# A linear-attention and feed-forward block on one core: one more tile transposed by DMA, projections cut in two, the whole order rewritten

## The chip, the cores and the metric

The kernel runs on one core of one Trainium2 chip. A core has five engines that run side by side and meet through semaphores: TensorE (PE; its weight loads are shown as PEld), VectorE (DVE), ScalarE (ACT), GpSimd (POOL) and SyncE (SP, which here only issues DMAs; ACT issues a few too). Results of TensorE land in PSUM, eight banks of 512 fp32 columns per partition; everything else lies in SBUF. The metric is device time in microseconds (us), the median of several runs.

## The reference

One transformer block over 2048 tokens of width 640, in bf16:

```
h  = x + attention(layernorm(x)) @ wo
h2 = h + silu(layernorm(h) @ w1) @ w2        # hidden width 1728
attention: q, k, v = x @ wqkv, 32 heads of 20
  phi_q = [softmax(q w_phi), softmax(-q w_phi)]      (40 features per head)
  phi_k = the same of k
  kv = sum over tokens of phi_k^T v ;  z = sum of phi_k
  out = (phi_q kv) / (phi_q z)
```

The sums over all tokens (`kv`, `z`) must be complete before the first token's attention output can be formed, so the kernel has a key/value half and an output half.

## The kernel before, in words

The 2048 tokens are 16 tiles of 128. Tiles 0 to 3, 4 to 7, 8 to 11 and 12 to 15 share one transposed buffer `XnT` each. Nothing is scheduled by a planner at build time: the string `ORDER` is the program. Each word is a step, `name.arguments@banks`; a loop at the end of the kernel calls `op_name` with the arguments, and `banks` says which PSUM banks the step takes. Every engine executes its instructions in the order in which the words issue them. Waits for data, for a free PSUM bank and for a free buffer are set by the framework. SP's DMAs also take turns on eight completion semaphores, so each waits for the DMA eight places ahead of it.

The words that matter here (line numbers of the kernel before; `t` a tile, `g` a group of tiles):

- Loads: `lx` (x), `lk`, `lv` (key and value weights), `lp` (phi), `l1`, `l2`, `lh`, `lo` (later weights), all L236; `lq.c` (L251) loads and transposes a piece of the query weights.
- Warm-up: `wm` (L268) are products of constants whose results nobody reads.
- Weights: `wt.c` (L322) transposes a piece of the key weights on PE, `wc.c` copies it out of PSUM (`v` on DVE, `a` on ACT). `ph` (L198) spreads phi on DVE. `fk.c` (L337) multiplies both, so that the key projection gives `k w_phi` at once; `fc.c` casts the result into `Wfk` (L171 on ACT). `gk`, `gc` are the same for the query weights (`Wfq`).
- Layer norm of x: `st.t` (L273, L274) takes mean and variance on DVE, in two halves of 320 columns and an aggregation; `rs` (L278 to L289) makes the reciprocal root, a power on POOL (L281), and the shift (L283); `xn.t` normalises, on DVE (L297) or ACT (L302).
- Transposing x: either `xt.t` on PE (L308, five transposes) with a copy `xc.t`, or `xd.t`, one DMA transpose from SP (L315).
- Keys and values: `kp.t` and `vp.t` (L370), ten products each, 5 pieces of the contraction times 2 halves; `ke.t` (L395) takes both exponentials on ACT, `vc.t` copies the values. `kr.t` (L403, L406) sums and inverts on DVE, `kn.t` (L414, L418) multiplies, on POOL, or shared with DVE (`p` all on POOL, `q` three quarters, `b` half, `d` a quarter, `v` none). `cc.t` (L427) adds the tile to `kv`, 32 small products into bank 7.
- The join: `kc`, `km` (L441 to L445) turn `kv` into a block-diagonal operand `KVBD`, with the mask that `mc`, `mt` make.
- Queries: `qp`, `qs` (first part) and `qr`, `qt` (second part) are the products of four tiles with a piece of `Wfq` (L457), `qe` the exponentials on ACT (L479).
- Output of the attention: `dp.t` (L504), 40 small products into four banks; `dw.t` (L522 to L528) and `dr.t` (L533) divide on DVE; `do` scales (L539, POOL or DVE), `td.t` transposes by DMA (L559), `op.t` multiplies by `wo` (L566), `oa.t` adds to x (L575).
- Feed-forward: `sq`, `sr`, `hn`, `hd` normalise and transpose h; `up.g.k` (L645, L655) and `ua` (Silu, L667) make the hidden layer of a group of tiles, `yp`, `yh` (L691, L704) the second product, `yo` and `yz` add and store.

Two lines set the shape of the projections and of the statistics:

```
ps[:, half, 0:320], tok(XnT[t // GT], t)[:, c, :], W[:, c, half * 320 : (half + 1) * 320],
nc.vector.bn_stats(stats[:, k, :], X[:, t, k * 320 : (k + 1) * 320])
```

Of the kernel before, what the change touches and what calls it, by code (L numbers as in the profile page):

```python
# [31 lines left out]
rs.10.12 xn.8.a vc.2.a vc.1.a kp.2@0 ke.2 st.4 xd.9 st.5 kp.3@4 lo.0.2.s ke.3 rs.4.6 vp.3@2 xn.11.v vp.9@6  # L32
vc.9.a xn.4.a kp.9@0 ke.9 vc.3.a st.12 st.13 st.6 rs.12.14 xd.8 kr.1 kn.1.p kp.8@4 ke.8 mc.1 xn.13.a xn.12.a
xd.11 vp.11@6 vp.8@0 vc.8.a xn.5.v kr.0 kp.11@2 lq.2.s ke.11 st.7 rs.6.8 xn.6.a st.14 st.15 rs.14.16 xd.4
kr.9 vp.4@4 vc.4.a xd.5 vp.5@0 kn.0.p vc.11.a kr.2 vc.5.a kn.9.p kp.5@2 kr.11 kn.11.p gk.2@4 xn.10.a gc.2.a
xd.12 vp.12@6 vc.12.v kr.3 kn.3.p kp.4@0 xn.15.a ke.4 kp.12@4 cc.9 cc.1 kr.4 kn.4.p cc.0 xn.14.v cc.11 ke.5
kr.5 kn.2.d xd.13 ke.12 kr.12 lq.4.s xd.6 kp.6@0 lq.0.s ke.6 vp.13@2 vc.13.a kp.13@4 ke.13 vp.6@0 xd.15
xd.10 gk.4@2 vp.10@4 vc.6.a lq.3.s gk.3@0 gc.4.a gc.3.a vc.10.a kn.5.q kp.10@2 kn.12.p kr.6 xn.7.a l1.3.s
kn.6.q lq.1.s gk.1@0 gc.1.a kr.13 kn.13.p cc.4 cc.5 l1.0.s ke.10 kr.10 cc.2 cc.3 cc.12 xd.14 xd.7 kr.8
kn.8.p kn.10.d vp.15@4 vc.15.a kp.15@0 ke.15 kp.14@2 gk.0@4 gc.0.a vp.7@0 ke.14 kr.14 kn.14.p qp.0.1@4  # L40
# [6 lines left out]
dp.4@0 dw.4.p td.2 sq.0 qp.2.2@5 qs.2.2 qe.2.2 op.1@6 oa.1 sr.0 qp.2.1@4 dp.6@0 dw.6.p l1.5.s l1.1.s qs.2.1  # L47
qr.2.1 hn.0.a hd.0 sq.1 qt.2.1 sr.1 hn.1.v hd.1 qe.2.1 op.3@6 oa.3 sq.3 dp.5@0 dw.5.p op.2@4 sr.3 oa.2
hn.3.a sq.2 dr.5 do.5.0.p do.5.1.p qp.3.1@6 qs.3.1 l2.0.2.s l2.8.10.s qr.3.1 dp.9@0 dw.9.p td.5 dr.9
do.9.0.p dr.6 do.6.1.p dr.4 do.4.1.p do.4.0.p td.4 qt.3.1 qe.3.1 up.0.2@4 ua.0.2 dp.7@0 sr.2 up.0.0@6 ua.0.0  # L50
dw.7.p dr.7 up.0.3@4 ua.0.3 do.6.0.p dp.8@0 dw.8.p dr.8 hn.2.a up.0.1@6 ua.0.1 td.6 do.8.0.p op.5@4 oa.5
dp.12@0 dw.12.p dr.12 yp.1.0@6 do.7.1.p do.7.0.p sq.5 td.7 hd.3 op.4@4 oa.4 sr.5 hn.5.v hd.5 do.9.1.p sq.4
td.9 sr.4 hn.4.a dp.10@0 dw.10.p yp.1.1 yp.0.1@4 yh.0.0 hd.2 hd.4 yo.1 dp.11@0 dw.11.p dr.11 do.8.1.p
do.11.0.p td.8 yp.0.0 yo.0 op.7@6 oa.7 sq.7 dr.10 op.6@0 oa.6 sq.6 sr.6 op.9@2 up.1.6@4 do.11.1.v td.11 oa.9
sq.9 dp.15@0 ua.1.6 sr.9 up.1.5@6 ua.1.5 up.1.1@4 hn.9.v hd.9 do.10.0.p dw.15.p dr.15 hn.6.v hd.6 op.8@6
oa.8 sq.8 op.11@0 ua.1.1 sr.7 hn.7.v hd.7 up.1.3@2 oa.11 do.12.1.p sr.8 hn.8.v do.15.0.p dp.14@4 dw.14.p
dr.14 do.14.0.v hd.8 ua.1.3 up.1.4@0 ua.1.4 do.14.1.v td.14 up.1.0@2 sq.11 sr.11 hn.11.v ua.1.0 up.2.6@4
ua.2.6 dp.13@0 dw.13.p dr.13 do.13.1.p up.2.0@6 up.2.5@4 ua.2.5 op.14@0 up.1.2@2 ua.2.0 oa.14 sq.14 up.2.2@4
ua.1.2 do.12.0.p td.12 sr.14 op.12@6 oa.12 ua.2.2 hn.14.v do.10.1.p do.15.1.v yp.4.0@0 up.2.4@2 ua.2.4 td.10
op.10@4 oa.10 up.2.1@6 sq.12 sr.12 hn.12.a hd.11 hd.12 up.2.3@2 ua.2.1 yp.2.0@4 ua.2.3 yp.9.0@6 do.13.0.p  # L60
td.13 hd.14 yh.2.1@2 td.15 yh.1.0 yp.2.1 yo.2 yp.9.1 yo.9 op.13@4 yp.4.1 yo.4 sq.10 sr.10 yp.6.0@6 op.15@0
hn.10.v hd.10 oa.15 sq.15 sr.15 oa.13 hn.15.a hd.15 yp.7.1 yp.7.0 yo.7 yp.3.0@0 yp.5.0@4 yh.1.1 yh.2.0@2
sq.13 sr.13 yp.6.1 yo.6 yp.3.1 yp.5.1 yo.5 hn.13.v up.4.1@6 hd.13 up.4.2@4 yp.8.1 yp.8.0 ua.4.2 yo.3
up.3.0@0 ua.3.0 yo.8 up.3.3@2 ua.3.3 up.3.5@4 ua.3.5 up.4.0@0 ua.4.0 up.3.1@2 ua.3.1 ua.4.1 up.3.2@4 ua.3.2
up.4.3@0 ua.4.3 yp.14.0@2 yp.15.0@6 up.3.4@4 up.3.6@0 yh.4.0 yp.15.1 ua.3.4 ua.3.6 yp.11.0@4 yp.12.1@0 yo.15
yp.14.1 yo.14 yp.10.1@6 yh.3.1@2,3 yh.3.0 yp.10.0 yo.10 yp.12.0 yo.12 yp.11.1 yo.11 yp.13.0 yz.13.0.s
yp.13.1 yz.13.1.a
"""

@with_exitstack  # L70
def kernel(
# [194 lines left out]
    def op_wm(n=512):  # L266
        one = nc.const_aps.tensor
        nc.tensor.matmul(mm1()[:, 0:n], one(1.0, (P, P), BF16), one(1.0, (P, n), BF16), start=True, stop=True)  # L268

    def op_st(t):  # L270
        stats = sm.tile([P, 2, 6], F32, name="stats")
        for k in range(2):
            nc.vector.bn_stats(stats[:, k, :], X[:, t, k * 320 : (k + 1) * 320])  # L273
        nc.vector.bn_aggr(MV[:, t, :], stats[:])  # L274

    def op_rs(a, b):
# [86 lines left out]
            tl["gk", ce][:, 1, 0:320].rearrange("p (k r f) -> p k r f", k=2, r=C),  # L363
        )

    def proj(t, W):
        ps = mm2()
        for c in range(C):
            for half in range(2):
                nc.tensor.matmul(  # L370
                    ps[:, half, 0:320], tok(XnT[t // GT], t)[:, c, :], W[:, c, half * 320 : (half + 1) * 320],
                    start=(c == 0), stop=(c == C - 1),
                )
# [384 lines left out]
```

## Time and profile before

| | us |
|---|---|
| median of 3 runs (lowest, highest) | 236.49 (236.43, 236.63) |
| the profiled execution | 236.35 |
| its span, first to last instruction | 234.4 |
| PE busy in it | 230.5 (98%) |
| DVE, ACT, POOL busy | 133.5, 114.5, 95.4 |

The profile is of one execution. A row of a group gives the line, the engine, the operation, the tiles written and read, the shape and the count, then the busy time, the mean length of one in ns, and the idle time in front with what ended it. A row of the timeline or of the chain begins with its start in us from the first instruction, then its length. Lengths in the timeline are from the start of the first to the end of the last instruction of the row; since instructions of an engine overlap a little, the distance between two starts is often less than a length. A wait row gives the total, the number of waits and the longest.

### The profile page before, as it was taken

How to read it: one execution, taken by the hardware profiler on the slowest of the kernel's cores; microseconds unless marked ns; L12 is line 12 of the kernel's file. 1: busy time of each engine (PE TensorE's matmuls, PEld its weight loads, DVE VectorE, ACT ScalarE, POOL GpSimd, SP SyncE). 2: the span in 40 equal slices, each digit the busy share in tenths (PEclk: the TensorE clock that was granted, in tenths of full speed). 3: DMA queues.
4: the chain of work that ended last, by engine and by line, in shares of the span. 5: the costliest groups of instructions: out<-in, count | busy, mean ns of one | idle time of the engine just before them, and what ended most of it. 6: DMA issues, size and time to landing. Idle time of an engine off the chain costs nothing.

```text
span 234.4 us, 6307 instructions
## 1 busy us (share of the span) xinstructions
PE 230.5 (98%) x2674; PEld 148.4 (63%) x2674; DVE 133.5 (57%) x249; ACT 114.5 (49%) x171; POOL 95.4 (41%) x190
## 2 busy tenths in 40 slices
...
DMA packets 44844, 20.67 MB, mean 88 GB/s; under 512 B 34448, under 2 KB 44304, under 8 KB 44816
## 3 DMA queue, kind: packets, MB, share of 16 engines
...
q10 hardware_dynamic: 1088, 0.39, 0.8%
...
## 4 chain that ended last, share of the span: by engine, by line
PE 98%; ACT 1%; DVE 0%; issue 0%
PE mm L691 24%; PE mm L645 24%; PE mm L370 19%; PE mm L457 10%; PE mm L566 9%; PE mm L504 3%; PE mm L268 2%; PE mm L427 2%; PE mm L337 1%; PE mm L655 1%; PE mm L704 1%; ACT EqT L479 1%; PE mm L322 1%; PE mm L308 0%; DVE ob L721 0%
## 5 line engine op out<-in xcount | busy, mean ns | idle before, releaser
L691 PE MATMUL mm<-w,shT 128*128 128x320 bf16 (+2 forms) x416 | 58.7, 299 | 0.0
L645 PE MATMUL mm<-HnT,w 128*128 128x512 bf16 (+1 forms) x325 | 58.6, 337 | 0.0
L691 PEld LDWEIGHTS <-shT 128*128 128x128 bf16 x416 | 39.6, 98 | 17.2 <-issue 1.1
L667 ACT ACTIVATE shT<-mm 128x1024 bf16<-128x1024 f32 (+2 forms) x29 | 27.6, 963 | 44.6 <-PE mm L645 43.1
L712 DVE TENSOR_TENSOR ob<-mm,X 128x640 bf16<-128x640 f32 x15 | 12.3, 819 | 62.3 <-PE mm L691 59.3
L645 PEld LDWEIGHTS <-w 128*128 128x128 bf16 x325 | 31.4, 98 | 23.2
L370 PEld LDWEIGHTS <-XnT 128*128 128x128 bf16 x320 | 30.8, 98 | 12.0
L414 POOL TENSOR_TENSOR Ek<-Ek,Sk 128x1280 bf16<-128x1280 bf16 (+2 forms) x15 | 32.9, 2217 | 4.0 <-DVE Sk L406 4.0
L539 POOL TENSOR_TENSOR o<-u,rd 128x320 bf16<-128x320 f32 x28 | 19.9, 727 | 22.9 <-DVE rd L533 16.4
L583 ACT ACTIVATE sq<-X 128x640 bf16<-128x640 bf16 x16 | 11.7, 732 | 28.3 <-DVE X L575 27.2
L566 PE MATMUL mm<-wo,ot 128*128 128x320 bf16 x160 | 23.9, 299 | 0.3 <-ACT EqT L479 0.3
L457 PE MATMUL mm<-XnT,Wfq 128*128 128x512 bf16 x100 | 23.8, 380 | 0.0
L370 PE MATMUL mm<-wv,XnT 128*128 128x320 bf16 x160 | 23.7, 299 | 0.0
L370 PE MATMUL mm<-Wfk,XnT 128*128 128x320 bf16 x160 | 23.5, 299 | 0.0
L395 ACT ACTIVATE Ek<-mm 128x640 bf16<-128x640 f32 x32 | 20.5, 714 | 6.0 <-PE mm L370 5.1
L403 DVE TENSOR_REDUCE Sk<-Ek 128x64 f32<-128x1280 bf16 x16 | 23.2, 1452 | 0.3 <-ACT Ek L395 0.3
L479 ACT ACTIVATE EqT<-mm 128x1024 bf16<-128x1024 f32 (+1 forms) x24 | 19.7, 879 | 4.9 <-PE mm L457 4.8
L575 DVE SCALAR_TENSOR_TENSOR X<-mm,X 128x640 bf16<-128x640 f32 x16 | 13.0, 818 | 15.4 <-PE mm L566 15.1
L566 PEld LDWEIGHTS <-ot 128*128 128x128 bf16 x160 | 15.7, 98 | 7.3 <-issue 0.2
L273 DVE BATCH_NORM_STATS2 stats<-X 128x6 f32<-128x320 bf16 x32 | 13.6, 467 | 3.8 <-DMA X<-in_A_x_dram 3.8
L457 PEld LDWEIGHTS <-Wfq 128*128 128x128 bf16 x100 | 9.1, 98 | 9.3
L525 DVE TENSOR_TENSOR u<-mm,w 128x672 f32<-128x672 f32 x16 | 13.7, 857 | 1.2 <-DVE w L523 0.3
...
## 6 DMA issues: line engine op xcount, KB each, us to landing
...
X<-in_A_x_dram SPq DMA_DIRECT2D x3, 640.0 KB, 7.8
...
```

The lines of the kernel that those rows point to most:

```text
L370: nc.tensor.matmul(ps[:, half, 0:320], tok(XnT[t // GT], t)[:, c, :], W[:, c, half * 320 : (half + 1) * 320], start=(c == 0), stop=(c == C ...
L395: nc.scalar.activation(Ek[:, s, :].rearrange("p (a n) -> p a n", a=2), tl["kp", t][:, :, 0:320], AF.Exp, scale=1.0 - 2.0 * s,)
L403: nc.vector.tensor_reduce(Sk[:], tl["ek", t][:].rearrange("p s (h f) -> p (s h) f", f=DH), axis=AX.X, op=ALU.add,)
L414: nc.gpsimd.tensor_tensor(Ek3[:, 0:n], Ek3[:, 0:n], Sk[:, 0:n].unsqueeze(2).to_broadcast([P, n, DH]), op=ALU.mult,)
L457: nc.tensor.matmul(tl["qp", g, i][:, k, :], Wfq[:, c, r * P : (r + 1) * P], XnT[g][:, c, :], start=(c == 0), stop=(c == C - 1),)
L479: nc.scalar.activation(E[:, s, rs[0] : rs[-1] + 1, :], tl["qp", g, i][:, 0 : len(rs), :], AF.Exp, scale=1.0 - 2.0 * s,)
L525: nc.vector.tensor_tensor(u[:], A[1][:, :, :, 0:21], w[:].unsqueeze(3).to_broadcast([P, 4, 8, 21]), op=ALU.mult,)
L539: (nc.vector if eng == "v" else nc.gpsimd).tensor_tensor(tl["o", t][:, a * 320 : (a + 1) * 320].rearrange("p (h f) -> p h f", f=DH), tl["u ...
L566: nc.tensor.matmul(ps[:, half, 0:320], tl["ot", t][:, c, :], wo[:, c, half * 320 : (half + 1) * 320], start=(c == 0), stop=(c == C - 1),)
L645: nc.tensor.matmul(ps[:, i * W : (i + 1) * W], w1[:, c, fc * P : (fc + 1) * P], HnT[g][:, c, 0:W], start=(c == 0), stop=(c == C - 1), skip ...
L667: nc.scalar.activation(sh[:, a:b], tl["up", g, k][:, 0 : b - a], AF.Silu)
L691: nc.tensor.matmul(ps, shT[g][:, fc * W + i * P : fc * W + (i + 1) * P], w2[:, fc, a:b], start=first and fc == 0, stop=last and fc == FC - ...
```

## The change

The order is written anew for every engine, with other PSUM banks and with some steps on other engines. What is computed, the shapes of the products and the buffers are the same. In particular:

- `xt.3` and `xc.3` (five transposes on PE, a copy on ACT) are replaced by `xd.3`, one DMA transpose.
- `kp`/`vp` now issue the first three of the five contraction pieces, and new words `kq`/`vq` the last two, so other work can stand between them.
- `st` is cut into `sa` (first half of the columns) and `st` (second half and aggregation).
- The first weight transposes stand in the order 0, 4, 1, 2, 3. Tile 0's normalisation and transpose go ahead of most of the weight folding; `xn.0` and `xc.0` move from DVE to ACT, `wc.1` from ACT to DVE.
- The load of tiles 12 to 15 of x stands behind `lq.1` and `xd.3`.
- The kv sums stand in three blocks instead of four; of the multiplies `kn`, twelve instead of eleven are whole on POOL, one is halved.
- `hn`, `do` and `xn` change engines for a number of tiles.

```diff
-mk mo lx.0.1.a lk.0.1.s lp.a lx.1.2.s lk.4.5.a wm.512@7 wm.512@7 wm.512@7 wm.512@7 wm.512@7 wm.512@7
-wm.512@7 wm.512@7 wt.0@0 lk.1.2.s ta wc.0.a wm.256@2 wm.256@2 wm.256@2 wm.256@2 wm.256@2 wm.256@2 wt.1@1 wc.1.a st.0 rs.0.1
-ph.v fk.0@2 fc.0.a st.1 lk.2.3.s wt.2@4 wc.2.v lk.3.4.s wt.3@5 wc.3.v fk.1@6 fc.1.a rs.1.2 fk.2@0 fc.2.a
-lx.2.4.s xn.0.v lx.8.12.s wt.4@4 wc.4.v lv.0.3.s fk.3@2 fc.3.a xt.0@5 xn.1.v xc.0.v st.2 fk.4@6 fc.4.a
-rs.2.3 lv.3.5.s mc.0 xt.1@4 xc.1.a st.9 st.8 rs.8.10 lx.4.8.s st.3 rs.3.4 kp.0@0 ke.0 xn.2.a kp.1@2 ke.1
-lx.12.16.s vp.1@6 st.10 xt.2@5 vp.0@0 xc.2.a xn.9.a vc.0.a vp.2@2 st.11 lo.2.5.s xn.3.v xt.3@4 xc.3.a
...
-mt qe.0.2 cc.15 cc.14 kc km.0 lh.s qp.3.0@4 qs.3.0 qr.3.0 km.1 dp.0@0 l1.4.s close dw.0.p dr.0 qt.3.0
-do.0.1.p qe.3.0 qp.2.0@6 qs.2.0 qr.2.0 qt.2.0 qe.2.0 do.0.0.p dp.1@0 dw.1.p qp.1.0@4 dr.1 do.1.0.p qs.1.0
-qr.1.0 qt.1.0 qe.1.0 qp.1.1@6 td.0 do.1.1.p td.1 dp.3@0 dw.3.p dr.3 do.3.0.p qs.1.1 qr.1.1 qt.1.1 qe.1.1
-qp.3.2@4 qp.1.2@5 dp.2@0 dw.2.p qs.1.2 qe.1.2 do.3.1.p td.3 qs.3.2 op.0@6 dr.2 do.2.1.p do.2.0.p qe.3.2 oa.0
...
+lx.0.1.a mk mo lk.0.1.s lp.a wm.512@7 wm.512@7 wm.512@7 wm.512@7 wm.512@7 wm.512@7 wm.512@7 wm.512@7 wt.0@0
+sa.0 st.0 rs.0.1 lx.1.2.s sa.1 lk.4.5.a wm.256@2 wm.256@2 wm.256@2 wm.256@2 wm.256@2 wm.256@2 wt.4@1
+lk.1.2.s wt.1@2 ta ph.v st.1 wc.0.a fk.0@4 wc.1.v lk.2.3.s wt.2@3 rs.1.2 xn.0.a xt.0@6 wc.4.a wc.2.v
+lk.3.4.s wt.3@7 wc.3.v fc.0.a fk.1@0 xc.0.a fc.1.a fk.2@2 fc.2.a fk.3@4 xn.1.v xt.1@7 xc.1.a lx.2.4.s sa.2
+lx.8.12.s st.2 sa.3 rs.2.3 lv.0.3.s st.3 rs.3.4 fc.3.a xn.2.v kp.0@0 sa.8 sa.9 st.9 fk.4@2 fc.4.a kp.1@6
+sa.10 kq.1 kq.0 xn.3.a st.8 st.10 xt.2@4 xc.2.a vp.0@2 lv.3.5.s vq.0 sa.11 st.11 vc.0.a lx.4.8.s sa.4 lq.1.s
+xd.3 lx.12.16.s vp.1@4 vq.1 kp.2@2 kq.2 rs.8.10 xn.9.v xd.9 ke.0 vc.1.a ke.2 rs.10.12 xn.11.a vp.2@0 vq.2
...
+vq.15 vc.15.a cc.4 cc.7 qe.0.1 cc.10 cc.3 cc.13 cc.15 lo.0.2.s cc.14 kc km.0 qs.0.2 l2.0.2.s l2.2.4.s qs.3.0
+km.1 qr.3.0 qt.3.0 l1.0.s qe.0.2 dp.0@0 qp.2.0@6 qs.2.0 close dw.0.p qr.2.0 dr.0 do.0.0.p do.0.1.p td.0
+qe.3.0 qt.2.0 qe.2.0 qp.1.1@4 dp.1@0 qs.1.1 qr.1.1 qp.1.2@6 qs.1.2 qe.1.2 dw.1.p dr.1 do.1.1.p dp.3@0 dw.3.p
+qt.1.1 dr.3 do.3.0.v qe.1.1 do.1.0.p td.1 qp.1.0@6 qs.1.0 qr.1.0 qt.1.0 qe.1.0 dp.2@0 op.0@4 dw.2.p oa.0
+dr.2 qp.2.2@6 qs.2.2 qe.2.2 do.3.1.p dp.4@0 do.2.1.p dw.4.p sq.0 qp.3.2@7 qs.3.2 qe.3.2 sr.0 op.1@4 qp.2.1@6
+oa.1 sq.1 dp.6@0 dw.6.p qs.2.1 td.3 op.3@4 oa.3 qr.2.1 qt.2.1 do.2.0.p td.2 hn.0.a hd.0 dp.5@0 sr.1 hn.1.a
+qp.3.1@4 hd.1 dr.4 do.4.1.p dw.5.p dr.5 do.5.0.p dr.6 qe.2.1 do.6.1.p do.4.0.p qs.3.1 qr.3.1 qt.3.1 qe.3.1
+dp.9@0 dw.9.p op.2@6 oa.2 do.5.1.v dr.9 up.0.0@4 ua.0.0 dp.7@0 do.9.1.p dw.7.p dr.7 do.7.0.v do.7.1.v l1.5.s
...
+up.1.4@2 ua.1.4 up.1.6@4 dr.13 do.13.1.v ua.1.6 td.10 dp.14@0 op.10@6 oa.10 up.1.0@4 ua.1.0 dw.14.p hd.9
...
+    def op_sa(t):
+        tl["stats", t] = sm.tile([P, 2, 6], F32, name="stats")
+        nc.vector.bn_stats(tl["stats", t][:, 0, :], X[:, t, 0:320])
+
     def op_st(t):
-        stats = sm.tile([P, 2, 6], F32, name="stats")
-        for k in range(2):
-            nc.vector.bn_stats(stats[:, k, :], X[:, t, k * 320 : (k + 1) * 320])
+        stats = tl["stats", t]
+        nc.vector.bn_stats(stats[:, 1, :], X[:, t, 320:D])
         nc.vector.bn_aggr(MV[:, t, :], stats[:])
...
-    def proj(t, W):
-        ps = mm2()
-        for c in range(C):
+    def proj(t, W, ps, cs):
+        for c in cs:
...
     def op_vp(t):
-        tl["vp", t] = proj(t, wv)
+        tl["vp", t] = mm2()
+        proj(t, wv, tl["vp", t], range(3))
+
+    def op_vq(t):
+        proj(t, wv, tl["vp", t], range(3, C))
...
     def op_kp(t):
-        tl["kp", t] = proj(t, Wfk)
+        tl["kp", t] = mm2()
+        proj(t, Wfk, tl["kp", t], range(3))
+
+    def op_kq(t):
+        proj(t, Wfk, tl["kp", t], range(3, C))
```

More of the change, by code (lines that the diff above doesn't have):

```diff
@@ L31 @@
-lx.12.16.s vp.1@6 st.10 xt.2@5 vp.0@0 xc.2.a xn.9.a vc.0.a vp.2@2 st.11 lo.2.5.s xn.3.v xt.3@4 xc.3.a
[L32 to L40, printed above, removed]
@@ L41 @@
-qs.0.1 qr.0.1 kp.7@2 ke.7 l2.10.13.s kr.15 l1.2.s cc.8 vc.7.v cc.13 l2.2.4.s cc.10 qt.0.1 qp.0.0@2 qs.0.0
-kn.15.p qr.0.0 qt.0.0 qe.0.1 l2.4.6.s kr.7 kn.7.v l2.6.8.s qe.0.0 vp.14@0 vc.14.a qp.0.2@6 qs.0.2 cc.6 cc.7
-mt qe.0.2 cc.15 cc.14 kc km.0 lh.s qp.3.0@4 qs.3.0 qr.3.0 km.1 dp.0@0 l1.4.s close dw.0.p dr.0 qt.3.0
-do.0.1.p qe.3.0 qp.2.0@6 qs.2.0 qr.2.0 qt.2.0 qe.2.0 do.0.0.p dp.1@0 dw.1.p qp.1.0@4 dr.1 do.1.0.p qs.1.0
-qr.1.0 qt.1.0 qe.1.0 qp.1.1@6 td.0 do.1.1.p td.1 dp.3@0 dw.3.p dr.3 do.3.0.p qs.1.1 qr.1.1 qt.1.1 qe.1.1
@@ L46 @@
-qp.3.2@4 qp.1.2@5 dp.2@0 dw.2.p qs.1.2 qe.1.2 do.3.1.p td.3 qs.3.2 op.0@6 dr.2 do.2.1.p do.2.0.p qe.3.2 oa.0
[L47 to L65, printed above, removed]
@@ new lines @@
+lx.8.12.s st.2 sa.3 rs.2.3 lv.0.3.s st.3 rs.3.4 fc.3.a xn.2.v kp.0@0 sa.8 sa.9 st.9 fk.4@2 fc.4.a kp.1@6
+sa.10 kq.1 kq.0 xn.3.a st.8 st.10 xt.2@4 xc.2.a vp.0@2 lv.3.5.s vq.0 sa.11 st.11 vc.0.a lx.4.8.s sa.4 lq.1.s
+xd.3 lx.12.16.s vp.1@4 vq.1 kp.2@2 kq.2 rs.8.10 xn.9.v xd.9 ke.0 vc.1.a ke.2 rs.10.12 xn.11.a vp.2@0 vq.2
+vc.2.a kp.3@4 kq.3 sa.5 ke.3 mc.0 vp.3@2 vq.3 vc.3.a xd.11 sa.6 l1.3.s ke.1 gk.1@0 kp.9@4 kq.9 st.4 vp.9@2
+ke.9 vq.9 st.5 st.6 kp.11@6 kq.11 xn.8.v xd.8 sa.7 rs.4.6 xn.4.a st.7 rs.6.8 sa.13 vc.9.a gc.1.a xn.10.a
@@ new lines @@
+ke.11 vp.11@4 sa.12 st.12 st.13 rs.12.14 xn.5.v xn.7.a kp.8@2 kq.8 ke.8 xn.6.v l2.8.10.s kr.2 vq.11 vc.11.a
+vp.8@0 vq.8 vc.8.a xd.5 kp.5@6 kq.5 vp.5@2 vq.5 ke.5 lq.0.s xd.4 vp.4@4 xn.12.v xd.12 kr.1 kn.2.q xn.13.a
+kn.1.p kr.0 kn.0.p gk.0@0 vq.4 vc.4.a sa.15 st.15 vp.12@6 vq.12 sa.14 st.14 rs.14.16 xd.10 kr.5 gc.0.a
+vp.10@4 xd.6 kp.6@0 xn.15.a kn.5.p kq.6 vc.12.a kr.3 kn.3.p cc.2 cc.1 cc.0 vc.5.v cc.5 ke.6 l2.10.13.s xd.7
+kp.12@2 kq.12 kr.11 kn.11.p kr.8 kn.8.p kr.6 kn.6.p lo.2.5.s vq.10 vc.10.a xd.13 vp.13@0 vq.13 vc.13.a
```

24 lines of the change are left out of this document (21 added, 3 removed).

## The prediction

> **What bounds the kernel now.** I read the head of the page, then what PE waited for, then the chain of work that ended last.
>
> ```profile
> span 234.4 us, 6307 instructions
> PE 230.5 (98%) x2674; PEld 148.4 (63%) x2674; DVE 133.5 (57%) x249; ACT 114.5 (49%) x171; POOL 95.4 (41%) x190
> ...
> PE mm L268 <- PEq L742: 0.8, 1, 0.8
> PE mm L566 <- ACT EqT L479: 0.3, 1, 0.3
> ...
> 6.70 0.32 PE mm L337 x6
> ...
> 14.24 0.28 PE mm L308 x5
> 14.52 2.72 PE mm L370 x20
> ...
> 58.99 0.86 PE mm L427 x96
> ...
> 65.20 1.13 PE mm L427 x128
> ...
> 71.68 2.70 PE mm L457 x12
> ...
> 208.83 3.24 PE mm L645 x15
> ...
> 231.67 0.29 DVE ob L721
> ```
>
> TensorE (PE) is the bound. It is busy 230.5 of the 231.67 before the last addition; after its start-up the only listed wait is 0.3. What follows (last add, last store) is the same in both orders. So the time is PE's work plus PE's waits; only these two count, and a wait anywhere costs its full length. There is little to win: what the order could still take away is 0.3 plus part of the start-up. There is much to lose.
>
> Unit prices from these rows: a 320-column matmul 0.136 (2.72/20), a 512-column one 0.216 (3.24/15), five transposes 0.28, a fold 0.32. Before a block of small matmuls, 12 products take 2.70 instead of 2.59: 0.1 to enter such a block. Inside, a kv tile (32 matmuls) is 0.27 (1.13 less 0.86), so 0.86 for three leaves 0.05 to 0.1 to go out again: 0.15 to 0.2 a block.
>
> **Work removed from PE.** Tile 3 of x loses five transposes: 0.28. The kv sums stand in three blocks instead of four: 0.2. The last product of `up.1.6`, a half-array one, is now followed by `dp.14` instead of a full-array product: one change of form less, 0.1. Sum -0.58 (bounds -0.4 to -0.6). Splitting key and value products 3+2 changes no matmul.
>
> If transposes cost PE their whole length, not their distance, the five would be worth more:
>
> ```profile
> L308 PE MATMUL mm<-ident,xn 128*128 128x128 bf16 x20 | 1.8, 219 | 0.0
> ```
>
> That would be 5 x 0.219 = 1.1, and the end 0.8 earlier. The chain's 0.28 for five speaks against it; I give it 2 in 100. The Trainium skill ("TensorE: Matmul & The Clock Gate", Part 4) has about 275 ns for a PE transpose in a kernel; by that the gain would be an estimated 1.4, which the trace's 0.28 for five contradicts.
>
> **The start, where the order costs.** In 0 to 13 us (time order, all engines):
>
> ```profile
> 5.08 0.99 DVE L198 TENSOR_TENSOR phb<-phr,mask 128x800 bf16<-128x800 bf16 x1
> 5.24 1.24 POOL L281 TENSOR_TENSOR RS<-RS,nhalf 128x1 f32<-128x1 f32 x1 [0.75 <-DVE RS L278]
> 6.58 0.26 POOL L283 TENSOR_SCALAR RS<-MV,RS 128x1 f32<-128x1 f32 x1
> 6.74 0.69 ACT L171 COPY wTk<-mm 128x640 bf16<-128x640 bf16 x1 [1.07 <-PE mm L322]
> 7.33 3.17 ACT L171 CAST Wfk<-mm 128x640 bf16<-128x640 f32 x5
> 8.20 0.44 DVE L297 TENSOR_SCALAR xn<-X,MV,RS 128x640 bf16<-128x640 bf16 x1
> 9.45 0.48 DVE L169 COPY XnT<-mm 128x640 bf16<-128x640 bf16 x1
> 9.99 2.89 PE L370 MATMUL mm<-Wfk,XnT 128*128 128x320 bf16 x20
> 10.35 0.74 ACT L171 COPY XnT<-mm 128x640 bf16<-128x640 bf16 x1
> 11.24 0.55 POOL L281 TENSOR_TENSOR RS<-RS,nhalf 128x1 f32<-128x1 f32 x1 [1.66 <-DVE RS L278]
> 12.72 1.52 PE L370 MATMUL mm<-wv,XnT 128*128 128x320 bf16 x10
> 15.43 0.92 ACT L302 ACTIVATE xn<-X,RS 128x640 bf16<-128x640 bf16 x1
> 16.25 0.67 ACT L171 CAST Vp<-mm 128x640 bf16<-128x640 f32 x1
> ```
>
> Before: by 12.72 PE has done the five weight transposes, the five folds (`fk`), tiles 0 and 1 of x, and both their key products. ACT's share from 6.74 on was `wc.1`, five casts (`fc`) and `xc.1`; `xn.0` and `xc.0` were DVE's (8.20, 9.45).
>
> After: `xn.0` and `xc.0` are ACT's, ahead of the casts that the key products need. ACT's queue from there: `xn.0, wc.4, fc.0, xc.0, fc.1, fc.2, xc.1, fc.3, fc.4`. Distances from start to start: `xn` 0.82 (15.43 to 16.25), a copy 0.59 (6.74 to 7.33), a cast 0.60 ((10.35 - 7.33)/5). `xn.0` can't start before POOL has both statistics, 6.84. So `fc.4` starts at 6.88 + 0.82 + 3 x 0.59 + 4 x 0.60 = 11.87, lasts 0.7 and ends at 12.58. Behind each stands PE in program order: `xt.0` at 7.85, where PE is ready at 7.3 (from about 6.0: two transposes, a fold, a transpose), `kp.0` at 10.2 instead of 9.8 (its bank is freed by `fc.1`), and the last part of `kq.1` at 12.63. Then 6 matmuls (0.82) finish `kq.1` and `kq.0` at 13.44, with the same work done as before by 12.72: **+0.72**. That `wt.4`, not `wt.1`, now comes second may bring it forward a little, which these waits swallow.
>
> Bounds: the 1.24 of POOL's power ran beside DVE's `phb`; later ones take 0.55. New is half of tile 1's statistics ahead of `phb`, so `phb` runs at about 5.5 to 6.5. If the power then takes 0.55, the statistics stand at 6.15, `fc.4` ends at 11.88 and the key products at 12.74: +0.02. If `phb` merely pushes POOL's second step behind itself, 7.05: +0.9. I take 6.84, as the trace has it; it lies between. The Trainium skill ("SBUF — State Buffer", Who interferes with whom) says that a VectorE instruction with two SBUF inputs and a GpSimd one that reads SBUF exclude each other, whoever starts first. The long power beside `phb` agrees; by it the power now goes first and `phb` delays the second step, the +0.9 case, ending 0.2 later than I say.
>
> **Tile 3 by DMA and SP's queue.** `xn.3` ends on ACT at about 13.4.
>
> ```profile
> XnT<-xn SPq DMA_TRANSPOSE x12, 2.7
> ...
> X<-in_A_x_dram SPq DMA_DIRECT2D x3, 640.0 KB, 7.8
> ```
>
> It lands 2.7 after its issue, 16.1; `kp.3` comes at 19.1: hidden by 3. Behind this wait on SP stands the load of tiles 12 to 15, issued at 14.7 instead of 6.4. At the listed 7.8 it lands at 22.5; DVE wants tile 13 at about 21.7: at worst DVE is 0.8 late, which its queue absorbs (next part). Nothing on PE.
>
> **20 to 68 us: normalisation of the key exponents.** Each tile needs DVE's sum and reciprocal, then POOL's (or shared) multiply, and the kv blocks wait for them.
>
> ```profile
> 24.16 2.36 POOL L414 TENSOR_TENSOR Ek<-Ek,Sk 128x1280 bf16<-128x1280 bf16 x1 [1.45 <-DVE Sk L406]
> ...
> 31.07 1.43 DVE L403 TENSOR_REDUCE Sk<-Ek 128x64 f32<-128x1280 bf16 x1
> 33.00 1.43 DVE L403 TENSOR_REDUCE Sk<-Ek 128x64 f32<-128x1280 bf16 x1
> ...
> 38.47 12.72 POOL L414 TENSOR_TENSOR Ek<-Ek,Sk 128x1280 bf16<-128x1280 bf16 x6 [0.67 <-DVE Sk L406]
> ```
>
> 1.93 a tile on DVE (31.07 to 33.00, with its reciprocal), 2.12 to 2.36 on POOL. POOL now has twelve whole tiles instead of eleven. DVE starts `kr.2` at about 24.4 (behind statistics and `xn`); then 16 x 1.93 = 30.9, two tiles' statistics 2.0, one `xn`, one value copy and three parts of multiplies 3.8, and about 2.3 waiting for the last tiles' exponentials: `kr.14` ends at 63.4 and `kn.14`'s POOL half (1.2 to 1.6) by 65.0; `cc.14` comes at about 65.8. Cost 0, cover 0.8. Were the multiplies as long as in the 24 us stretch (2.36) everywhere, and DVE blocked by them in turn, PE would wait about 1.0.
>
> **68 to 100 us: attention.** `dp` uses four banks that DVE must read before the next `dp` there; each query product must be drained by ACT before its banks return.
>
> ```profile
> L457 PE MATMUL mm<-XnT,Wfq 128*128 128x512 bf16 x100 | 23.8, 380 | 0.0
> ...
> 71.22 0.47 PE L504 MATMUL mm<-KVBD,EqT 32*128 32x44 bf16 x40
> 71.61 2.76 PE L457 MATMUL mm<-XnT,Wfq 128*128 128x512 bf16 x12
> 71.77 0.36 DVE L522 RECIPROCAL w<-mm 128x32 f32<-128x32 f32 x1 [0.33 <-PE mm L504]
> 73.28 0.85 DVE L528 TENSOR_TENSOR u<-u,mm 128x672 f32<-128x672 f32 x1
> 73.98 1.94 ACT L479 ACTIVATE EqT<-mm 128x1024 bf16<-128x1024 f32 x2 [0.72 <-PE mm L457]
> 74.31 0.47 PE L504 MATMUL mm<-KVBD,EqT 32*128 32x44 bf16 x40
> ...
> 88.29 1.52 PE L566 MATMUL mm<-wo,ot 128*128 128x320 bf16 x10 [0.27 <-ACT EqT L479]
> ```
>
> From the start of a `dp` DVE needs its banks until 73.28 + 0.85 = 74.13; with 0.04 to PE that is 2.95 from `dp` to `dp`. A query product ends 0.16 after its slot (0.380 less 0.216); with 0.03 to ACT, 1.94 for its two exponentials and 0.04 back, its banks return 2.17 after its last slot. Before, PE had 3.09 between two `dp` (74.31 - 71.22), of which `dp` is 0.39 and the change of form 0.1; the one wait is the 0.3 at 88. In the new order:
> - `dp.1` to `dp.3`: 0.39 + 10 products (2.16) + 0.1 = 2.65 against 2.95: 0.30 (half of it already at `qp.1.2`, whose banks `qt.2.0` left 2.03 earlier).
> - `qp.2.2` takes the banks of `qt.1.0` after `dp.2` and `op.0`: 0.1 + 0.39 + 1.36 = 1.85 against 2.17: 0.32.
> - `qp.2.1` waits for `qe.3.2`, which ACT does behind `sq.0`: 0.1.
> - `dp.5` to `dp.9`: `qp.3.1` to `qt.3.1`, again 2.65 against 2.95: 0.30.
>
> Sum 1.0. Behind each wait stands all of PE's queue, and with it DVE and ACT, which have no other source of work. What goes is the 0.3 at 88: there `op.2` needed the banks of the exponentials just started; now `dp.9` and `op.2` take others. Net **+0.7** (bounds -0.3, if engines run a little ahead of these differences, to +0.8).
>
> **After 100 us** I laid PE's unit prices end to end in both orders and compared the time between each step and its reader. From the second group on, `op` to its `up` is 14.5 or more where it was 8.3; `up` to its first `yp` is 1.2 to 3.5 where it was 0 to 3.5, and the piece that comes late is read only some matmuls into the `yp`. Cost 0; a miss costs what the largest attention wait does, 0.3.
>
> **The sum**, against the profiled execution (236.35: span 234.4 and 1.95 around it): -0.58 + 0.72 + 0.7 = +0.84, 237.2. The median of the runs is 0.14 above that execution: **237.3**. About 0.5 (0.2%) is what a measurement can tell from no change.
>
> **Rivals.** (A) POOL's power is not delayed, and the start costs 0.02: 236.6, not slower. For it speaks the 0.55 row, against it that `phb` then falls on POOL's next step. It decides from statistics that stand by 6.2. (B) The attention waits are absorbed: 237.3 - 1.0 = 236.3. For it, each is at most 0.3; against, each is a difference of quoted rows. A and B together: 235.6, and the change does what a new order is for. (C) The multiplies on POOL come late and `cc.14` waits 1.0: 238.3. For it, the cover of only 0.8 at the end of a queue of 40 us; against, the 2.12 of six in a row.
>
> **Chances.** Forecast 0.44, A 0.17, B 0.12, both 0.12, C 0.15. Faster by over 0.2% are both, and the lower edges of A and B: 0.2. Within: the rest of A and B, 0.22. Slower: forecast and C, 0.58. The range goes from both to a little beyond C, 235.5 to 238.5; the forecast's own is 236.8 to 237.8.
>
> **What would show it.** PE idle at 7.3 to 7.8 and 9.8 to 10.2 waiting for ACT's `xn` and `Wfk`; the first value product at 14 behind `xt.2`; four or five waits of 0.1 to 0.3 on ACT's `EqT` or DVE's `u` between 70 and 95; none at `kp.3`. I am wrong if POOL's first power takes 0.6, if PE waits for POOL's `Ek` near 65, or if a wait stands after 100.

## The result, and the profile after

The kernel after takes 238.31 us (median of 4 runs, 237.97 to 238.53) against 236.46 (4 runs, 236.23 to 236.63) for the kernel before: a ratio of 1.0078 (95% interval 1.0066 to 1.0090), or 1.85 us slower. The forecast was 237.3, slower by 0.8, with 235.5 to 238.5 as its range. The sign holds and the time lies in the range, but the loss is more than twice the forecast's, and the forecast's own band, 236.8 to 237.8, is missed.

The profiled execution of after took 238.21, 1.86 more than that of before. Head of its page, its waits of PE (total, number, longest), and the end of its chain of waits:

```profile
span 236.2 us, 6306 instructions
PE 230.0 (97%) x2669; PEld 147.3 (62%) x2669; DVE 130.9 (55%) x250; ACT 115.8 (49%) x173; POOL 95.2 (40%) x188
...
PE mm L327 <- DMA wk<-in_A_wqkv_dram: 0.8, 1, 0.8
PE mm L313 <- ACT xn L307: 0.3, 1, 0.3
PE mm L515 <- DVE u L539: 0.3, 1, 0.3
PE mm L374 <- ACT Wfk L173: 0.2, 1, 0.2
PE mm L577 <- DMA ot<-o: 0.2, 1, 0.2
PE mm L468 <- ACT EqT L490: 0.2, 1, 0.2
PE mm L438 <- POOL Ek L425: 0.2, 1, 0.2
...
233.32 0.29 DVE ob L732
```

The last addition starts at 233.32 instead of 231.67: 1.65 of the 1.86 are PE's. Its waits now come from every side: ACT, DVE, POOL and a DMA. The list shows only the idle time behind an instruction's modelled end; a wait is longer than that. In the following it is measured from start to start of PE's instructions, less what their form takes elsewhere (0.216 for 512 columns, 0.136 for 320, 0.095 more ahead of a block of small ones). Timeline of after, the rows that carry the difference:

```profile
5.47 0.54 POOL L286 TENSOR_TENSOR RS<-RS,nhalf 128x1 f32<-128x1 f32 x1 [0.99 <-DVE RS L283]
5.71 0.97 DVE L200 TENSOR_TENSOR phb<-phr,mask 128x800 bf16<-128x800 bf16 x1
6.13 0.69 POOL L288 TENSOR_SCALAR RS<-MV,RS 128x1 f32<-128x1 f32 x1
6.85 0.92 ACT L307 ACTIVATE xn<-X,RS 128x640 bf16<-128x640 bf16 x1 [1.69 <-POOL RS L288]
7.82 0.45 PE L313 MATMUL mm<-ident,xn 128*128 128x128 bf16 x5 [0.33 <-ACT xn L307]
10.17 1.03 PE L374 MATMUL mm<-Wfk,XnT 128*128 128x320 bf16 x6 [0.23 <-ACT Wfk L173]
13.36 0.44 PE L313 MATMUL mm<-ident,xn 128*128 128x128 bf16 x5
...
63.48 0.55 DVE L417 RECIPROCAL Sk<-Sk 128x64 f32<-128x64 f32 x1
64.17 0.82 DVE L429 TENSOR_TENSOR Ek<-Ek,Sk 128x640 bf16<-128x640 bf16 x1
66.18 0.38 PE L438 MATMUL mm<-Ek,Vp 128*21 128x40 bf16 x32 [0.16 <-POOL Ek L425]
...
72.51 2.46 PE L468 MATMUL mm<-XnT,Wfq 128*128 128x512 bf16 x10
75.07 0.46 PE L515 MATMUL mm<-KVBD,EqT 32*128 32x44 bf16 x40
78.78 1.53 PE L577 MATMUL mm<-wo,ot 128*128 128x320 bf16 x10
80.48 1.24 PE L468 MATMUL mm<-XnT,Wfq 128*128 128x512 bf16 x5 [0.16 <-ACT EqT L490]
89.01 2.33 PE L468 MATMUL mm<-XnT,Wfq 128*128 128x512 bf16 x10
91.65 0.46 PE L515 MATMUL mm<-KVBD,EqT 32*128 32x44 bf16 x40 [0.30 <-DVE u L539]
...
107.10 1.52 PE L577 MATMUL mm<-wo,ot 128*128 128x320 bf16 x10
108.80 1.40 PE L577 MATMUL mm<-wo,ot 128*128 128x320 bf16 x9 [0.18 <-DMA ot<-o]
```

How to read them. At 13.36 PE has done what it had done by 12.72 before. At 66.18 the last key-value tile waits for POOL. From 72.51 to 75.07, 10 query products take 2.56 where their form takes 2.16 + 0.095: 0.3 of waiting. From 78.78 to 80.48, an output product takes 1.70 where it takes 1.36: 0.33. From 89.01 to 91.65: 0.37. From 107.10 to 108.80: 0.34, now for an output transpose; one of 0.18 stands ahead of it at 103.46. (Each wait is taken between two neighbouring instructions and unrounded, so it can differ by 0.01 or 0.02 from the sums of these rows.) What each stage cost PE, against before:

| us | forecast | measured |
|---|---|---|
| start, to the same work done | +0.72 | +0.64 |
| 36 to 68: sums over tokens | 0 | +0.34 (one new wait) |
| 68 to 95: attention | +0.70 | +0.71 (1.05 of new waits, the 0.34 at 88 gone) |
| after 95 | 0 | +0.52 (two waits for output transposes) |
| work removed (what is left over) | -0.58 | -0.57 |
| sum on PE | +0.84 | +1.64 |
| behind PE's last matmul | 0 | +0.22 |

### The profile page after: what moved, and what is told of

Its sections match the earlier page's. It is cut to its first block, busy times and chain, and to the rows that moved or that the text cites. A ratio compares the mean times of both kernels' runs of the same rounds, so it can differ in the third digit from the quotient of the medians.

```text
span 236.2 us, 6306 instructions
## 1 busy us (share of the span) xinstructions
PE 230.0 (97%) x2669; PEld 147.3 (62%) x2669; DVE 130.9 (55%) x250; ACT 115.8 (49%) x173; POOL 95.2 (40%) x188
## 4 chain that ended last, share of the span: by engine, by line
PE 79%; POOL 6%; DVE 4%; DMA 4%; ACT 3%; issue 2%; POOLq 0%; ACTq 0%; DVEq 0%
PE mm L656 24%; PE mm L702 23%; PE mm L374 16%; PE mm L577 7%; POOL Ek L425 3%; DMA ot<-o 3%; PE mm L468 2%; PE mm L515 2%; DMA X<-in_A_x_dram 1%; PE mm L666 1%; PE mm L715 1%; DVE u L536 1%; DVE u L539 1%; ACT Ek L406 1%; POOL o L550 1%
## 5 line engine op out<-in xcount | busy, mean ns | idle before, releaser
L425 POOL TENSOR_TENSOR Ek<-Ek,Sk 128x1280 bf16<-128x1280 bf16 (+3 forms) x16 | 35.1, 2219 | 4.9 <-DVE Sk L417 4.9
L550 POOL TENSOR_TENSOR o<-u,rd 128x320 bf16<-128x320 f32 x23 | 17.2, 762 | 33.1 <-DVE rd L544 28.4
L374 PE MATMUL mm<-Wfk,XnT 128*128 128x320 bf16 x160 | 24.5, 299 | 0.2 <-ACT Wfk L173 0.2
L577 PEld LDWEIGHTS <-ot 128*128 128x128 bf16 x160 | 15.2, 98 | 7.4 <-DMA ot<-o 0.9
L539 DVE TENSOR_TENSOR u<-u,mm 128x672 f32<-128x672 f32 x16 | 13.6, 853 | 0.6
```

The lines of the kernel that those rows point to most:

```text
L374: nc.tensor.matmul(ps[:, half, 0:320], tok(XnT[t // GT], t)[:, c, :], W[:, c, half * 320 : (half + 1) * 320], start=(c == 0), stop=(c == C ...
L425: nc.gpsimd.tensor_tensor(Ek3[:, 0:n], Ek3[:, 0:n], Sk[:, 0:n].unsqueeze(2).to_broadcast([P, n, DH]), op=ALU.mult,)
L550: (nc.vector if eng == "v" else nc.gpsimd).tensor_tensor(tl["o", t][:, a * 320 : (a + 1) * 320].rearrange("p (h f) -> p h f", f=DH), tl["u ...
L577: nc.tensor.matmul(ps[:, half, 0:320], tl["ot", t][:, c, :], wo[:, c, half * 320 : (half + 1) * 320], start=(c == 0), stop=(c == C - 1),)
```

## The experiments

All times are medians in us; "before" is the kernel before, run beside it.

| run | time | before | ratio (95%) |
|---|---|---|---|
| xd3_alone | 237.66 | 236.56 | 1.0051 (1.0039 to 1.0063) |
| start_back | 238.92 | 236.56 | 1.0101 (1.0085 to 1.0117) |
| early_new | 237.14 | 236.56 | 1.0030 (1.0018 to 1.0041) |
| late_new | 238.07 | 236.56 | 1.0066 (1.0052 to 1.0081) |
| l2_early | 237.47 | 236.19 | 1.0054 (1.0042 to 1.0066) |
| kn14 | 237.59 | 236.19 | 1.0066 (1.0050 to 1.0081) |
| phb_later | 237.42 | 236.19 | 1.0050 (1.0037 to 1.0063) |
| dp_shift | 238.05 | 236.19 | 1.0101 (1.0069 to 1.0133) |
| after_again | 237.99 | 236.33 | 1.0063 (1.0044 to 1.0082) |
| three | 236.96 | 236.33 | 1.0028 (1.0015 to 1.0040) |
| better | 238.57 | 236.33 | 1.0087 (1.0068 to 1.0106) |
| xt3_thrice | 236.57 | 236.33 | 1.0011 (1.0000 to 1.0021) |

After was run twice: 1.85 slower than before, and 1.66 (after_again). Gains over after below are taken against both, each run by its distance from the before that was run beside it.

**Where the loss stands: two halves.** early_new has after's order up to the first `dp`, late_new from there.

```diff
 early_new: after up to  ... qr.3.0 qt.3.0 l1.0.s qe.0.2 | before from  dp.0@0 close dw.0.p ...
 late_new:  before up to ... qs.3.0 qr.3.0 km.1 qt.3.0   | after from   dp.0@0 qp.2.0@6 ...
```

> The order of after up to the first dp, the order of before from there (weight loads shared out so that each is loaded once). Theory (PE's work and waits of the two stretches add up): the first stretch costs 0.81 at the start and 0.21 at the key-value blocks, less 0.28 for the transposes and 0.2 for one block: 0.54 slower than before, about 237.0. Rival (queues of DVE and ACT carry lateness over the seam, so that the stretches are not separable): off that by more than 0.4, and new waits of PE in the attention.

> The order of before up to the first dp (its products cut 3 and 2 but left side by side, and tile 3 transposed on PE), the order of after from there. Theory: waits of 1.05 in the attention less the 0.34 of before, 0.52 on the output transposes after 100 us, less 0.1 for a change of form: 1.1 slower than before, about 237.6. Rival (the attention waits come from DVE and ACT arriving late from after's first stretch): they shrink here, and the time is within 0.5 of before. Cutting the products 3 and 2 with nothing between should cost nothing: PE's first 67 us as in before.

```profile
71.96 0.46 PE L513 MATMUL mm<-KVBD,EqT 32*128 32x44 bf16 x40 [0.42 <-DVE u L537]
```

early_new lost 0.58, where the theory had 0.54, but not at the places that it named. Its PE ended 0.73 late. Only 0.28 of that stands ahead of the first `dp` (68.81 against 67.88, with three 512-column products more done by then); most of the rest is the wait shown, 0.49 from start to start, for DVE's `u` just behind the seam, which neither kernel has there. So the rival's sign showed, and that the time agrees is in part luck. (The 0.81 for the start in these expectations is 0.64 to the same work done.) late_new's PE ended 1.08 late, where 1.1 was said: 0.13 sooner at the first `dp`, 1.21 lost behind it. The attention's waits are 0.25, 0.33 and 0.37 without after's first half, and one of 0.47 stands on an output transpose. So the attention's waits belong to that order and are not lateness handed on. Its median lost 1.5, more than its profiled execution (1.2), with runs from 237.4 to 238.5.

**What five transposes cost PE.**

```diff
-xn.3.v xt.3@4 xc.3.a
+xn.3.v xt.3@4 xt.3@4 xt.3@4 xc.3.a
```

> The order of before with the five transposes of tile 3 on PE done three times over into the same bank, nothing else. Theory (0.28 for five): 0.56 slower than before. Rival (each costs PE its listed 0.22, or the about 0.275 that a kernel's PE transpose is put at): 2.2 to 2.75 slower.

```profile
16.72 1.00 PE L307 MATMUL mm<-ident,xn 128*128 128x128 bf16 x15
17.56 0.30 PE L369 MATMUL mm<-Wfk,XnT 128*128 128x320 bf16 x1
```

Fifteen transposes take 0.84 from start to start: 0.28 for five. The rival of 2.2 or more is out. The measured loss, 0.24 (0.0 to 0.5), is below 0.56. In the profiled execution PE needed 0.55 more than before from its first value product to its end, and the start happened to be 0.35 shorter; why the median shows only 0.24 is not settled.

**The transpose by DMA alone.**

```diff
-vc.0.a vp.2@2 st.11 lo.2.5.s xn.3.v xt.3@4 xc.3.a
+vc.0.a xn.3.v xd.3 vp.2@2 st.11 lo.2.5.s
```

> The order of before, with tile 3 of x normalised a little earlier and transposed by DMA instead of by PE, nothing else. Theory (five transposes cost PE the 0.28 they take in the chain of waits, and the DMA lands about when the key product of tile 3 needs it, at worst 0.1 late): 0.2 to 0.3 faster than before, about 236.2. Rival 1 (the transposes cost PE their whole length of 0.22 each): 1.1 faster, 235.4. Rival 2 (the DMA lands late, or holds up the transposes of tiles 8, 9 and 11 behind it on SP): no gain or slower, 236.5 to 237.0, with a wait of PE on the DMA of XnT between 18 and 22 us.

```profile
16.56 1.29 SPq L313 DMA_TRANSPOSE XnT<-xn  x1
...
19.27 1.53 PE L368 MATMUL mm<-Wfk,XnT 128*128 128x320 bf16 x10 [0.45 <-DMA XnT<-xn]
20.64 1.52 PE L368 MATMUL mm<-wv,XnT 128*128 128x320 bf16 x10
22.83 1.40 PE L368 MATMUL mm<-wv,XnT 128*128 128x320 bf16 x9 [0.66 <-DMA XnT<-xn]
```

Rival 2 held in kind, and cost more than its 237.0: 1.1 slower. The transpose is issued at 16.56, 0.6 late for its own product, and the next one behind it on SP is 0.8 late for its own. To win its 0.28, the normalised tile must be there at least 0.6 sooner; after has it some 3 us sooner than before (13.8 against 16.7). That is a likely reason for after's other start, and the next run shows that the two can't be had apart by simply going back.

```diff
-... wt.4@1 lk.1.2.s wt.1@2 ta ph.v st.1 ... xn.0.a xt.0@6 wc.4.a ... xc.0.a fc.1.a ... xt.1@7 xc.1.a ...
+... wt.1@1 wc.1.a sa.0 st.0 rs.0.1 ph.v fk.0@2 fc.0.a ... xn.0.v ... xc.0.v sa.2 st.2 ... xt.1@4 xc.1.a
+sa.3 st.3 rs.3.4 xn.2.v kp.0@0 sa.8 sa.9 st.9 kp.1@6 sa.10 kq.1 kq.0 xn.3.a st.8 st.10 xt.2@4 xc.2.a ...
```

> The order of after, but its start up to the copy of tile 1's transpose put back as before has it (normalisation and copy of tile 0 on DVE, statistics uncut there, folds before tile 0). Theory (the start costs PE 0.81 in the profile of after, 13.53 against 12.72 for the same work, and PE's waits add up): 0.8 faster than after, about 237.5. Rival (the later chain of exponentials, sums and multiplies sets when the key-value sums end, so an earlier start only makes the wait for POOL near 66 longer): at most 0.3 faster than after, 238.0 or more, with the wait at the last key-value block grown to about 0.8.

```profile
14.26 0.92 ACT L306 ACTIVATE xn<-X,RS 128x640 bf16<-128x640 bf16 x1 [3.58 <-POOL RS L287]
15.08 0.67 ACT L172 COPY XnT<-mm 128x640 bf16<-128x640 bf16 x1
...
15.80 0.98 PE L373 MATMUL mm<-wv,XnT 128*128 128x320 bf16 x6 [1.36 <-ACT XnT L172]
```

Both missed: 2.4 slower than before. PE is at the transposes of tile 2 at 12.65, 0.7 ahead of after (0.25 of it because the first tile of x came sooner), and then waits 1.5. ACT stood idle for 3.58 in front of tile 3's normalisation, whose statistics DVE now delivers late, and behind it in ACT's queue stands the copy of tile 2 that PE needs.

**What made the start late.**

```diff
-lk.1.2.s wt.1@2 ta ph.v st.1 wc.0.a
+lk.1.2.s wt.1@2 ta st.1 ph.v wc.0.a
```

> The order of after, with DVE's spreading of phi moved behind the second half of tile 1's statistics. Theory (POOL's second step on the statistics of tile 0 took 0.69 instead of 0.26 only because DVE's product of two SBUF operands ran beside it, and the normalisation of tile 0 on ACT starts when it ends): that step takes 0.26, the normalisation starts 0.4 earlier, and the key products of tiles 0 and 1 end 0.2 to 0.4 earlier; 238.0. Rival (the first fold now waits for phi, and the chain goes on from there): step 0.26, but no gain, 238.3 or a little slower.

```profile
5.23 0.54 POOL L284 TENSOR_TENSOR RS<-RS,nhalf 128x1 f32<-128x1 f32 x1 [0.75 <-DVE RS L281]
5.88 0.26 POOL L286 TENSOR_SCALAR RS<-MV,RS 128x1 f32<-128x1 f32 x1
...
12.75 0.44 PE L311 MATMUL mm<-ident,xn 128*128 128x128 bf16 x5
```

POOL's step takes 0.26 instead of 0.69, and the key products end at 12.75 instead of 13.36. Not all of this 0.61 is the edit's: POOL's power begins at 5.23 instead of 5.47, because the first tile of x came 0.24 sooner in this execution. The edit's own part is 0.37, as expected. The theory held. The median's gain over after is 0.4 to 0.6, and this profile also has none of after's waits for output transposes.

**The wait at 66.**

```diff
-kn.7.p kr.14 kn.14.b mc.1
+kn.7.p kr.14 kn.14.d mc.1
```

> The order of after, with only a quarter instead of half of the last multiply of tile 14 on POOL, the rest on DVE. Theory (PE's wait of 0.34 at the last key-value tile is for POOL's half, which takes 1.89 beside DVE's half; DVE is idle from 65.0): the wait goes or falls under 0.1, 0.3 faster than after, about 238.0. Rival (the wait is for the sum of tile 14 on DVE, and DVE's longer share ends as late): no change, 238.3.

```profile
L423 POOL TENSOR_TENSOR Ek<-Ek,Sk 128x320 bf16<-128x320 bf16 x1 | 1.7, 1687 | 0.0
```

The wait falls from 0.34 to 0.13 from start to start, too short for the list of waits, and the run is 0.25 to 0.45 faster than after. The theory held for most of it. The gain needn't all be this edit's, for this profile too has no wait for an output transpose. The quarter took POOL 1.69 beside DVE's three quarters, nearly as long as the half in after (1.90).

**The output transposes after 100 us.**

```diff
-do.7.1.v l1.5.s do.6.0.p ... sr.3 l2.4.6.s hn.3.v ... dw.12.p l2.6.8.s yp.1.0@6
+l2.2.4.s l2.4.6.s l2.6.8.s qs.3.0 ...
+do.7.1.v l1.5.s do.6.0.p ... sr.3 hn.3.v ... dw.12.p yp.1.0@6
```

> The order of after, with the two loads of the second feed-forward weight that stand among the output transposes (pieces 4 to 8) issued before the attention instead. Theory (the transposes of tiles 4 and 9 landed 5.6 and 4.4 after their issue, instead of 2.6, because those loads were under way; PE waited 0.18 and 0.35 for them): both waits go, 0.5 faster than after, about 237.8. Rival (the transposes queue behind each other, four of them within 8 us): the waits stay, 238.3.

From the view of the tile `ot`, time from issue to landing (shortest, median, longest) in 95 to 112 us of after:

```profile
DMA to landing us min/median/max: 2.6/3.4/5.6
```

in after_again, and its PE:

```profile
DMA to landing us min/median/max: 2.6/3.6/6.4
...
101.75 1.52 PE L577 MATMUL mm<-wo,ot 128*128 128x320 bf16 x10
104.09 1.53 PE L577 MATMUL mm<-wo,ot 128*128 128x320 bf16 x10 [0.82 <-DMA ot<-o]
```

and in l2_early:

```profile
DMA to landing us min/median/max: 2.6/3.2/4.8
```

and in 90 to 120 us of before:

```profile
DMA to landing us min/median/max: 2.6/2.6/2.9
```

Both waits are gone and l2_early is 0.4 to 0.6 faster than after. That speaks for the theory, but doesn't show it: one transpose still took 4.8, only it was issued earlier. In profiles with the loads in place the waits were 0.52 (after), 0.98 (after_again), 0.70 (dp_shift), 0.47 (late_new), and none (kn14, phb_later, start_back); without them, none in l2_early and three. The slowest transpose took 5.2 to 6.4 in the four with a wait, 4.7 to 5.1 in the three with the loads and no wait, and 4.5 and 4.8 in the two without loads. So the loads are not the whole cause. The rival of this run, that the transposes delay each other, is not excluded: in after they are issued 1.3 to 3.3 apart, in before, where none takes more than 2.9, 2.4 to 5.1. What delays them stays open.

> The kernel after, unchanged, beside the others. Theory (the start, the key-value block and the attention are waits on engines and repeat; the 0.52 after 100 us hangs on when two weight loads land): 1.5 to 1.9 slower than before; the waits before 95 us repeat within 0.1, those on the output transposes need not. Rival (all of it repeats): 1.85 slower, with the same two waits at 103 and 108.

The waits between 60 and 95 us repeated within 0.02, and the key products again ended late (13.12); the waits on the output transposes did not repeat, 0.98 at one place instead of 0.18 and 0.34 at two.

**Moving a wait in the attention.**

```diff
-qr.1.1 qp.1.2@6 qs.1.2 qe.1.2 dw.1.p dr.1 do.1.1.p dp.3@0 dw.3.p qt.1.1 dr.3
+qr.1.1 qt.1.1 qp.1.2@6 qs.1.2 qe.1.2 dw.1.p dr.1 do.1.1.p dp.3@0 dw.3.p dr.3
```

> The order of after, with the three query products of the last part of tile group 1, piece 1, moved ahead of the output products of tile 3, so that 13 and 10 query products stand in the two gaps instead of 10 and 13. Theory (DVE needs 2.95 from one of these blocks to the next, whichever they are): the waits of 0.13 and 0.18 ahead of tile 3 go, and one of about 0.3 comes ahead of tile 2; the time stays within 0.2 of after, 238.3. Rival (the waits are for the exponentials of ACT in those banks): they go and none comes back, 238.0.

```profile
76.91 2.92 ACT L488 ACTIVATE EqT<-mm 128x512 bf16<-128x512 f32 x4 [1.85 <-PE mm L466]
...
78.04 1.24 PE L466 MATMUL mm<-XnT,Wfq 128*128 128x512 bf16 x4 [0.77 <-ACT EqT L488]
```

The waits ahead of tile 3 go, and a worse one comes, for ACT and not for DVE: the next product takes the bank that was filled just ahead of the block, and ACT, idle for 1.85, can start on its exponentials only at 76.91. So DVE's 2.95 is not the only limit, as the theory had it; the time (238.05) stays that of after. The profiled execution took 240.3, held up besides by 1.4 for a transpose of x at 41, far ahead of the rows shown.

**The three repairs together.** The edits of l2_early, kn14 and phb_later in one kernel.

> The order of after with the three edits together: phi spread behind the statistics, the two weight loads ahead of the attention, a quarter instead of half of tile 14's multiply on POOL. Theory (waits of PE in different stages add up): what each gave alone, 0.6 + 0.6 + 0.3, so about 1.4 faster than after and 0.4 slower than before, with the attention's waits of about 1.05 left as they are. Rival (they overlap: an earlier start only lengthens a later wait): less than 1.0 faster than after.

1.0 to 1.2 faster than after, between theory and rival, though the profile's PE ends 1.4 earlier than after's (0.3 of it because the first tile of x came sooner). It is still 0.63 slower than before: what is left is the attention's 0.71 and some tenths that no run takes apart, less the 0.57 of removed work.

**A version meant to beat both.**

```diff
-xc.1.a st.9 st.8 rs.8.10 lx.4.8.s st.3 rs.3.4 kp.0@0
+xc.1.a st.3 rs.3.4 st.9 xn.3.v st.8 rs.8.10 mc.0 lx.4.8.s kp.0@0
...
-lx.12.16.s vp.1@6
+lx.12.16.s xd.3 vp.1@6
...
-l1.2.s cc.8 vc.7.v cc.13 l2.2.4.s cc.10 qt.0.1 ... qs.0.2 cc.6 cc.7
+l1.2.s vc.7.v l2.2.4.s qt.0.1 ... qs.0.2 cc.8 cc.13 cc.10 cc.6 cc.7
```

> The order of before with two edits: tile 3 transposed by DMA, its statistics and normalisation put ahead of those of tiles 8 and 9 so that the transpose can be issued at about 13.7 and land near 16.4; and the third block of key-value sums joined to the fourth. Theory (0.28 for five transposes and 0.15 to 0.2 for a block, nothing else changes): 0.4 faster than before. Rival (the tiles pushed back wait in their turn, as when the transpose was added without moving the statistics): same as before or slower, with a wait of PE on XnT near 20 us.

```profile
17.84 0.43 PE L368 MATMUL mm<-Wfk,XnT 128*128 128x320 bf16 x2 [0.82 <-ACT Vp L169]
...
60.87 0.81 PE L455 MATMUL mm<-XnT,Wfq 128*128 128x512 bf16 x3 [0.74 <-ACT Ek L393]
...
70.00 0.37 PE L502 MATMUL mm<-KVBD,EqT 32*128 32x66 bf16 x27 [0.63 <-issue]
```

2.2 slower. The transpose of tile 3 now lands in time, but tile 9's statistics are late; ACT's normalisation of it stands ahead of the value copy whose bank PE needs. And the block of sums taken away at 59 had been cover: without its 0.86, PE comes to a bank that ACT still reads (60.87). A third wait, 0.8 within the first `dp` (70.00), has no cause that the profile shows. No kernel tried here beats the one before.

## Why the prediction was right and wrong

All three signs that the prediction named for being wrong were seen: a first power of 0.54, a wait for `Ek` near 65, and waits after 100. That the time still lies in the range is owed to the range's width, which reaches a little beyond rival C.

- **Work removed, -0.58:** holds in sum (-0.57, as what is left over). The 0.28 for five transposes is shown by the trace of the run that tripled them, against the Trainium skill's 275 ns for each ("TensorE: Matmul & The Clock Gate", Part 4); from the last product ahead of a block of sums to the first behind it, the four blocks of before take 5.23 in all and the three of after 4.98 without their wait, 0.25 less where 0.2 was said. The change of form was not measured by itself, and the run that joined a block lost more than it saved.
- **Start, +0.72:** near in size (0.64, in part by luck) and right in its waits (`xt.0` at 7.82 for ACT's `xn`, said 7.85; `kp.0` at 10.17 for `Wfk`, said 10.2). The reason was only half right. POOL's power took 0.54, the sign named for being wrong; but then `phb` fell on POOL's next step, 0.69, and the statistics stood at 6.82, said 6.84. This is the bound case, 7.05, but milder. That the two figures agree is luck: the first tile of x stood ready at 4.07 in this execution and at 3.83 in the one of before. Counted from there, the statistics stood 0.26 sooner than said. The key products ended 9.29 behind that moment in after (9.29 to 9.30 in all six profiles with this start), 8.89 behind it in before's profile, and 8.53 to 8.55 in four others with before's start. So the order of the start costs 0.40 against the one and 0.75 against the others. The Trainium skill's rule ("SBUF — State Buffer", Who interferes with whom: a VectorE instruction with two SBUF inputs and a GpSimd one that reads SBUF exclude each other) had said which step would be held; phb_later agrees with it, 0.26 against 0.69. Rival A, a start not late, would have been one word away (12.75 in phb_later, 12.72 before, with x at 3.83 in both).
- **Tile 3 by DMA:** hidden in after, as said, though it landed 3.8 after its issue, at 17.6 (said 2.7 and 16.1). What the step left out is the price, as xd3_alone, start_back and better point to it: a normalised tile that early asks for another order around it.
- **Sums over tokens, cost 0 with a cover of 0.8:** wrong by 0.34. The last tile came at 65.83, said 65.8, but its multiply ended at 66.12, said 65.0. The sums and reciprocals ended at 64.03, said 63.4. And POOL's half took 1.90, said 1.2 to 1.6. The price was misread from the row of six multiplies in 12.72: its 2.12 each mixes sizes. Kept apart by shape, first before (30 to 38 us), then after (20 to 68 us):

```profile
L414 POOL TENSOR_TENSOR Ek<-Ek,Sk 128x1280 bf16<-128x1280 bf16 x3 | 7.0, 2357 | 0.0
```

```profile
L425 POOL TENSOR_TENSOR Ek<-Ek,Sk 128x1280 bf16<-128x1280 bf16 x12 | 29.0, 2438 | 3.9 <-DVE Sk L417 3.9
L425 POOL TENSOR_TENSOR Ek<-Ek,Sk 128x640 bf16<-128x640 bf16 x1 | 1.9, 1897 | 0.0
L425 POOL TENSOR_TENSOR Ek<-Ek,Sk 128x320 bf16<-128x320 bf16 x1 | 0.7, 722 | 0.0
```

  A whole one takes 2.36, and more beside a multiply on DVE. Rival C had the mechanism, at a third of its price.
- **Attention, +0.70:** right, 0.71. `dp.1` to `dp.3` 0.31 (said 0.30, 0.13 of it at `qp.1.2`, said 0.14), `qp.2.2` 0.33 (0.32), `dp.5` to `dp.9` 0.37 (0.30), 0.05 at `dp.1` (none), none at `qp.2.1` (0.1). These came as differences of rows and repeat in every run of this order: rival B is out.
- **After 100 us, cost 0:** the step that failed most, by 0.52. It compared steps with their readers, and never asked how long a DMA transpose takes there: at most 2.9 in before, up to 5.6 in after. The diff moves two weight loads from the first half to between the output transposes, and sets these closer together. The waits differ from run to run, and which of the two makes the transposes slow is not settled.
- **Behind PE, 0:** 0.22 more, in the span's end and outside it; not explained.

The missing 1.0 us is thus 0.52 and 0.34 of waits put at nothing, and the 0.22 behind PE, less the 0.08 by which the start was better.
